# Attention and two dense stages on one core: the outset and the periods of the attention in another order, six PSUM banks for scores, one for values, one for sums

## The chip, the cores and the metric

The kernel runs on one core of a Trainium2 chip. The metric is device time in microseconds (us), the median of the runs; all times below are in us. The engines are TensorE (PE; its weight loads are PEld), VectorE (DVE), ScalarE (ACT), GpSimd (POOL) and SyncE (SP, which here only issues DMAs).

## The reference

Softmax attention with a soft cap, then two dense stages. `B, H, S, D` = 2, 12, 448, 64; 896 tokens of width 768.

```python
scores = cap * np.tanh(scale * (q @ k.T) / cap)
attn = exp(scores - max); attn = attn / (sum(attn) + 1e-09)
x = (attn @ v) as (896, 768)
h = np.maximum(np.maximum(x @ w1, x @ w2), x @ w3)
x = h @ w_out
xn = x / rms(x) * rms_g
out = (silu(xn @ w_gate) * (xn @ w_val)) @ w_out2
```

## The kernel before

The attention is worked in 12 **pairs** of heads, one pair in a **period** of the software pipeline (`period(i)`, i = 0 to 12). Keys are cut into four blocks c = 0 to 3, of 128, 128, 128 and 64 keys; the two heads of a pair lie side by side in the PE array. In period i:

- PE computes the scores of pair i (`scores`, blocks 0 to 2 at L210, each into two PSUM banks, one for each head; block 3 at L217, both heads in one bank), seven banks in all, out of the pool `bank` of five. It then computes the values of pair i-1 (`values`, L247, into one bank of the pool `banko` of two) and the sums of its exponentials over the keys (`sum_all`, L253, two matmuls with a matrix of ones into the one bank `banks`).
- ACT takes the tanh of each score bank (L212, L218), which frees that bank, and then the exponentials of the pair in two instructions (`expo`, L222: e01 of blocks 0 and 1, e23 of blocks 2 and 3).
- POOL adds the exponentials of blocks 0, 1 and 3 (`sum_01` L226, `sum_3` L231), DVE those of block 2 (`sum_2` L235); `sum_all` waits for that.
- DVE divides: `norm(i-2)` takes the reciprocal of the bank of sums (L257) and multiplies the bank of values with it (L259), which frees both; `split_x` (L267, L268) cuts the result into two parts for the dense stage.

Tiles of the PE array have three shapes here, which the rows name: 64\*128 (scores of blocks 0 to 2: 64 rows, 128 columns), 64\*64 (scores of block 3, values of block 3) and 128\*64 (values of blocks 0 to 2, sums).

The dense stages (L277, L531) run as **groups** of 18 matmuls in a fixed list. They need the weights in **units** that are split into a high and a low part (`split_unit`, eight instructions, for units 0 and 1 all on DVE; L109 to L117). Unit 0 is split in period 0, unit 1 in period 1 ahead of the norms, unit 2 in `tail`. `tail` (period 12, the last pair's values) is issued after the 18 matmuls of group 0, so that groups 0, 1 and 2 surround the last values; they use units 0, 1 and 2. Each engine works its instructions in the order in which the program is written (`manual_schedule`); a wait for another engine holds all that stands behind it on its own engine. Banks of the dense stages come from the same three pools in turns of eight (`any_bank`).

Ahead of period 0 stand two **warm** matmuls on zeros (L316) that wait for no data.

Of the kernel before, what the change touches and what calls it, by code (L numbers as in the profile page):

```python
# [8 lines left out]
F32 = mybir.dt.float32  # L9
# [9 lines left out]
B, H, S, D = 2, 12, 448, 64  # L19
NP = H // 2  # L20
P = 128
CP = 112
NC = S // CP
# [17 lines left out]
def attn_moe_kernel(ctx, tc, bounded, qT, kT, v, cap, w123, wo, wgv, wo2, rms_g, out):  # L41
# [17 lines left out]
    def small(name, dt=F32):  # L59
        return tp.tile([P, 512], dt, tag="t", name=name, bufs=NT)  # L60
# [12 lines left out]
        return tp.tile([P, S], F32, tag="xs", name="xs", bufs=NX)  # L73

    def bank():
        return pp.tile([P, 512], F32, tag="b", name="bank", bufs=5)

    def bank_o():
        return pp.tile([P, 512], F32, tag="o", name="banko", bufs=2)

    def bank_s():
        return pp.tile([P, 512], F32, tag="s", name="banks", bufs=1)
# [3 lines left out]
    def any_bank():  # L86

        turn[0] = (turn[0] + 1) % 8
        return (bank_s if turn[0] == 0 else bank_o if turn[0] in (3, 6) else bank)()

# [8 lines left out]
        sp.dma_start(out=mid.rearrange("p a b -> p (a b)").bitcast(U16)[:, :4 * U - 2], in_=src.bitcast(U16)[:, 1:4 * U - 1])  # L99
        return raw[:, :, 1], mid[:, :, 0]  # L100

    def split_unit(words, on_dve):
        hi, lo = (gp.tile([P, U], F32R, tag="g", name=name, bufs=NG) for name in ("whi", "wlo"))
        f = wp.tile([P, U], U32, tag="f", name="f", bufs=2)
        d = wp.tile([P, U], U32, tag="d", name="d", bufs=1)
        high, mid = words
        ff = f.bitcast(F32)
        steps = [
            (lambda: dve.tensor_scalar(f, high, 0x7FFFFFFF, None, op0=ALU.bitwise_and)) if on_dve else  # L109
            (lambda: act.activation(ff, high.bitcast(F32), AF.Abs)),  # L110
            lambda: dve.tensor_scalar(ff, ff, W_MIN, W_MAX, op0=ALU.max, op1=ALU.min),  # L111
            lambda: dve.tensor_scalar(f, f, 3, 0x3FFFF000, op0=ALU.logical_shift_left, op1=ALU.bitwise_and),
            lambda: dve.scalar_tensor_tensor(f, high, 0xC0000000, f, op0=ALU.bitwise_and, op1=ALU.bitwise_or),  # L113
            lambda: (dve.tensor_copy if on_dve else act.copy)(hi, ff),  # L114
            lambda: dve.tensor_scalar(d, f, 0xFF800000, None, op0=ALU.bitwise_and),  # L115
            lambda: dve.tensor_scalar(mid, mid, 0x01FFFFFF, None, op0=ALU.bitwise_and),
            lambda: dve.scalar_tensor_tensor(lo, mid, 2.0 ** -36, d.bitcast(F32), op0=ALU.mult, op1=ALU.mult),  # L117
            load_next,
        ]
        for step in steps:  # L120
            step()
        return hi, lo

    unit_src = [w123[j, n] for j in range(KC) for n in range(3)]
# [7 lines left out]
        if len(loaded) < len(unit_src):  # L132
            loaded.append(load_unit(unit_src[len(loaded)]))

    def split_next():
        i = len(units)
        units.append(split_unit(loaded[i], i < 2))
        loaded[i] = None

    with tc.manual_schedule():  # L140

        pairs = [(b, hp) for b in range(B) for hp in range(NP)]
        n = len(pairs)
        kq, vt, E, EX, Ssum, SB, PO, XS = {}, {}, {}, {}, {}, {}, {}, {}
        X = [None] * KC

        def load_pair(i):
# [88 lines left out]

        def values(i, *blocks):
            for c in blocks:
                if c == 0:
                    PO[i] = bank_o()  # L240
                for j in range(2):
                    if c < KB:
                        w, e = vt[i][:, c * P + j * D:c * P + (j + 1) * D], E[i][c][:, j, :]
                    else:
                        rows = slice(j * KL, (j + 1) * KL)
                        w, e = vt[i][rows, KB * P:], E[i][c][rows]
                    pe.matmul(PO[i][64 * j:64 * j + 64, :S], w, e, start=(c == 0), stop=(c == KB))  # L247

        def sum_all(i):

            ps = SB[i] = bank_s()
            for j in range(2):
                pe.matmul(ps[64 * j:64 * j + 64, :S], ones, Ssum[i][:, j, :], start=True, stop=True)  # L253

        def norm(i):
            r = small("r")[:, :S]
            dve.reciprocal(r, SB.pop(i)[:, :S])  # L257
            xs = XS[i] = spare()
            dve.tensor_mul(xs, PO.pop(i)[:, :S], r)  # L259

        def split_x(i):
            b, hp = pairs[i]
# [49 lines left out]
        dve.memset(warm, 0.0)  # L312
        act.activation(tsc, warm[:, :1], AF.Exp)
        ps = bank()
        for _ in range(2):
            pe.matmul(ps[:, :S], warm[:, :P], warm, start=True, stop=True)  # L316
        load_next()
        load_pair(1)
# [12 lines left out]
        if bounded:  # L331

            guard = const.tile([P, 1], F32, name="guard")
            dve.tensor_scalar_mul(guard, cap_sb, -1.0)
            dve.tensor_tensor(guard, guard, cap_sb, op=ALU.min)
            act.activation(guard, guard, AF.Exp)
            dve.tensor_scalar_mul(guard, guard, 1e-9 / P)
            def period(i):

                if i + 2 < n:
                    load_pair(i + 2)
                    load_v(i + 2)
                if i >= 2:
                    norm(i - 2)
                if i == n:
                    sum_3(i - 1, dve)
                if i >= 1:
                    sum_2(i - 1)  # L350
                if i == 1:
                    split_next()
                if i >= 2:
                    split_x(i - 2)
                if i < n:
                    for c in range(NC):
                        scores(i, c)
                if i >= 1:
                    values(i - 1, 0, 1, 2)
                    sum_all(i - 1)  # L360
                    values(i - 1, 3)
                if i < n:
                    expo(i)
                    if i == 0:

                        split_next()
                        sum_01(i, dve)
                        sum_3(i, dve)
                    else:
                        sum_01(i, dve if i == n - 1 else pool)  # L370
                        if i < n - 1:
                            sum_3(i, pool)

            def tail():
                period(n)
                split_next()
                norm(n - 1)
                split_x(n - 1)

            for i in range(n):  # L380
                period(i)
        else:
            for i in range(n):
                if i + 2 < n:
                    load_pair(i + 2)
                    load_v(i + 2)
                attend(i)
            for _ in range(3):
                split_next()
# [217 lines left out]
```

## Time and profile before

| | us |
|---|---|
| median of 3 runs (lowest, highest) | 554.96 (554.73, 556.86) |
| profiled execution, its own time | 556.08 |
| its span, first to last instruction | 554.3 |
| PE busy | 539.7 (97%) |
| DVE busy | 415.0 (75%) |
| ACT busy | 240.6 (43%) |
| POOL busy | 59.2 (11%) |

The attention takes the first 107 us of the span, up to group 0; the dense stages take the rest. "Granted clock" is the share of TensorE's full clock of 2.4 GHz that it was given: 1.00, or 0.50 for 1.2 GHz. Its record begins at 11.4 us; ahead of that the durations of matmuls tell the level. A matmul of float32 shows as two records (two passes). A busy PE is one with a matmul under way, and not one at its best pace.

### The profile page before, as it was taken

To read this page: it belongs to the slowest core of one execution; us is meant where nothing else is said; L and a number is where in the kernel's file an instruction comes from. 1 tells how busy PE (TensorE), PEld (TensorE's weight loads), DVE (VectorE), ACT (ScalarE), POOL (GpSimd) and SP (SyncE) were. 2 spreads that over 40 slices of the span, in tenths; PEclk is the share of its full clock that TensorE was granted. 3 is DMA by queue.
4 is the path that set the end of the run, shared out by engine and by line. 5 is a ranking of instruction groups with operands and counts; after the bars stand their busy time and mean duration, and the time that the engine had idled before them with its cause. 6 is when DMAs were issued, how large, how long until landed. Compare 5 with 4: busy or idle time off the path is not lost.

```text
span 554.3 us, 7037 instructions
## 1 busy us (share of the span) xinstructions
PE 539.7 (97%) x2682; PEld 438.3 (79%) x2682; DVE 415.0 (75%) x592; ACT 240.6 (43%) x347; POOL 59.2 (11%) x48
## 2 busy tenths in 40 slices
PE   7879999999999999999999999999999999999996
PEld 3223333479889999988998999988888999999996
DVE  4996777799998898686586888878777778836701
ACT  4858898714434333335454333333333333312201
POOL 0335556300000000002122000000000000000000
PEclk9889999999999999999999999999999999999999
DMA  7843320037897878566500476666666666874402
GB/s 256 340 157 100 101 94 6 1 115 246 319 316 287 294 246 278 197 247 229 187 0 1 139 264 245 217 215 207 210 218 223 223 219 217 318 275 173 156 1 105
DMA packets 24810, 105.90 MB, mean 191 GB/s; under 512 B 3008, under 2 KB 9408, under 8 KB 24768
## 3 DMA queue, kind: packets, MB, share of 16 engines
q1 hardware_dynamic: 23760, 104.19, 54.0%
q10 hardware_dynamic: 1008, 1.18, 0.6%
q8 instruction: 23, 0.38, 0.3%
q14 instruction: 19, 0.16, 0.1%
HBM read 102.60 MB, written 2.75 MB: 190 GB/s over the span
## 4 chain that ended last, share of the span: by engine, by line
PE 96%; ACT 1%; DMA 1%; DVE 1%; SPq 0%; issue 0%
PE bank L277 40%; PE banko L277 16%; PE bank L531 10%; PE banko L247 8%; PE banks L277 7%; PE bank L210 6%; PE banko L531 3%; PE banks L531 2%; PE bank L217 2%; PE banks L253 2%; DMA qv<-in_qT 1%; DVE sum L235 1%; ACT e L222 1%; ACT e L212 0%; SPq L600 0%
## 5 line engine op out<-in xcount | busy, mean ns | idle before, releaser
L114 ACT CAST whi<-f 128x768 fp32r<-128x768 f32 x58 | 48.8, 841 | 150.7 <-DVE f L113 127.9
L277 PE MATMUL bank<-xn,whi 128*128 128x512 f32 (+1 forms) x360 | 102.9, 367 | 0.0
L277 PE MATMUL bank<-x,whi 128*128 128x512 f32 (+2 forms) x276 | 79.2, 368 | 0.0
L277 PEld LDWEIGHTS bank<-xn,whi 128*128 128x128 f32 x360 | 66.5, 188 | 8.2
L277 PE MATMUL bank<-xn,wlo 128*128 128x512 f32 (+1 forms) x180 | 66.2, 368 | 0.0
L117 DVE SCALAR_TENSOR_TENSOR wlo<-mid,d 128x768 fp32r<-128x768 uint32 x60 | 58.3, 972 | 5.1 <-PE banks L277 1.6
L113 DVE SCALAR_TENSOR_TENSOR f<-raw,f 128x768 uint32<-128x768 uint32 x60 | 57.5, 959 | 2.1
L277 PEld LDWEIGHTS bank<-x,whi 128*128 128x128 f32 x276 | 51.0, 188 | 7.4 <-issue 1.4
L531 PE MATMUL bank<-whi,a 128*128 128x384 f32 x216 | 54.8, 334 | 0.0
L110 ACT ACTIVATE f<-raw 128x768 f32<-128x768 f32 x58 | 52.6, 907 | 3.5 <-DMA raw<-in_wo 2.5
L277 PE MATMUL bank<-x,wlo 128*128 128x512 f32 (+2 forms) x138 | 50.8, 368 | 0.0
L111 DVE TENSOR_SCALAR f<-f 128x768 f32<-128x768 f32 x60 | 34.8, 581 | 17.4 <-ACT f L110 16.3
L212 ACT ACTIVATE e<-bank,tsc 128x448 f32<-128x448 f32 x72 | 39.3, 642 | 18.8 <-PE bank L210 12.0
L257 DVE RECIPROCAL r<-banks 128x448 f32<-128x448 f32 x12 | 35.5, 2955 | 11.3 <-PE banks L253 11.3
L247 PE MATMUL banko<-e,qv 128*64 128x448 f32 (+1 forms) x192 | 43.2, 572 | 0.0
L277 PE MATMUL banko<-xn,whi 128*128 128x512 f32 (+1 forms) x144 | 40.7, 364 | 0.0
L210 PE MATMUL bank<-qv,k 64*128 64x448 f32 x144 | 37.1, 607 | 2.5 <-ACT e L212 1.9
L531 PEld LDWEIGHTS bank<-whi,a 128*128 128x128 f32 x216 | 39.0, 188 | 0.0
L222 ACT ACTIVATE e<-e,cap_sb 128x1792 f32<-128x1792 f32 (+1 forms) x24 | 37.5, 1633 | 0.0
L115 DVE TENSOR_SCALAR d<-f 128x768 uint32<-128x768 uint32 x60 | 35.5, 592 | 2.0
L277 PEld LDWEIGHTS bank<-xn,wlo 128*128 128x128 f32 x180 | 33.8, 188 | 4.0
L531 PE MATMUL bank<-wlo,a 128*128 128x384 f32 x108 | 36.1, 334 | 0.0
(130 smaller groups left out, 877.7 us busy)
## 6 DMA issues: line engine op xcount, KB each, us to landing
raw<-in_wgv SPq DMA_DIRECT2D x24, 768.0 KB, 4.2
mid<-in_wgv SPq DMA_DIRECT2D x24, 767.5 KB, 5.3
raw<-in_w SPq DMA_DIRECT2D x18, 768.0 KB, 5.2
raw<-in_wo SPq DMA_DIRECT2D x18, 768.0 KB, 4.2
mid<-in_w SPq DMA_DIRECT2D x18, 767.5 KB, 5.6
mid<-in_wo SPq DMA_DIRECT2D x18, 767.5 KB, 5.4
k<-in_kT SPq DMA_DIRECT2D x12, 224.0 KB, 3.1
qv<-in_qT SPq DMA_DIRECT2D x12, 224.0 KB, 3.5
```

Source lines behind the costliest of these rows:

```text
L110: (lambda: act.activation(ff, high.bitcast(F32), AF.Abs)),
L113: lambda: dve.scalar_tensor_tensor(f, high, 0xC0000000, f, op0=ALU.bitwise_and, op1=ALU.bitwise_or),
L114: lambda: (dve.tensor_copy if on_dve else act.copy)(hi, ff),
L115: lambda: dve.tensor_scalar(d, f, 0xFF800000, None, op0=ALU.bitwise_and),
L117: lambda: dve.scalar_tensor_tensor(lo, mid, 2.0 ** -36, d.bitcast(F32), op0=ALU.mult, op1=ALU.mult),
L210: pe.matmul(ps[j][:, :S], k_[rows, c * P:(c + 1) * P], q_[rows], start=True, stop=True)
L212: act.activation(t[:, j, :], ps[j][:, :S], AF.Tanh, scale=tsc)
L222: act.activation(e, e, AF.Exp, scale=cap_sb)
L247: pe.matmul(PO[i][64 * j:64 * j + 64, :S], w, e, start=(c == 0), stop=(c == KB))
L257: dve.reciprocal(r, SB.pop(i)[:, :S])
L277: pe.matmul(ps, a[:, k, :], x[k][h][:, cols], start=(k == 0 and n_ == 0), stop=(k == KC - 1 and n_ == 2))
L531: pe.matmul(acc_o[s][:, :HN], a[:, ts], w[:, sl], start=(k == 0 and n_ == 0), stop=(k == FC - 1 and n_ == 2))
```

## The change

- **Banks**: `bank` six, `banko` one, `banks` one. In the dense stages a bank still comes back after eight groups.
- **Outset**: three warm matmuls. In period 1 the scores of pair 1 and the values of pair 0 are interleaved. The split of unit 1 leaves period 1; its eight instructions and the DMA issue behind them (`load_next`, unit 3) are dealt out, one at the end of `split_x` in each of periods 2 to 8, the last with the issue in period 9.
- **Period**: values in the order 3, 0, 1, then the sums, then block 2.
- **Reciprocals**: the reciprocal of pair i-1 is written at the end of period i, not at the start of period i+1.

```diff
-        return pp.tile([P, 512], F32, tag="b", name="bank", bufs=5)
+        return pp.tile([P, 512], F32, tag="b", name="bank", bufs=6)
-        return pp.tile([P, 512], F32, tag="o", name="banko", bufs=2)
+        return pp.tile([P, 512], F32, tag="o", name="banko", bufs=1)
...
-        return (bank_s if turn[0] == 0 else bank_o if turn[0] in (3, 6) else bank)()
+        return (bank_s if turn[0] == 0 else bank_o if turn[0] == 7 else bank)()
...
+        def recip(i):
+            r = R[i] = small("r")[:, :S]
+            dve.reciprocal(r, SB.pop(i)[:, :S])
+
         def norm(i):
-            r = small("r")[:, :S]
-            dve.reciprocal(r, SB.pop(i)[:, :S])
             xs = XS[i] = spare()
-            dve.tensor_mul(xs, PO.pop(i)[:, :S], r)
+            dve.tensor_mul(xs, PO.pop(i)[:, :S], R.pop(i))
...
-        for _ in range(2):
+        for _ in range(3):
             pe.matmul(ps[:, :S], warm[:, :P], warm, start=True, stop=True)
...
-                if i == 1:
-                    split_next()
                 if i >= 2:
                     split_x(i - 2)
-                if i < n:
-                    for c in range(NC):
-                        scores(i, c)
+
+                    if i == 2:
+                        split_next(steps)
+                    for step in steps[:1 if i < 9 else None]:
+                        step()
+                    del steps[:1 if i < 9 else None]
+                if i == 1:
+                    scores(1, 0)
+                    scores(1, 1)
+                    values(0, 0, 1)
+                    scores(1, 2)
+                    scores(1, 3)
+                    values(0, 3)
+                    sum_all(0)
+                    values(0, 2)
+                else:
+                    if i < n:
+                        for c in range(NC):
+                            scores(i, c)
+                    if i >= 1:
+                        values(i - 1, 3, 0, 1)
+                        sum_all(i - 1)
+                        values(i - 1, 2)
                 if i >= 1:
-                    values(i - 1, 0, 1, 2)
-                    sum_all(i - 1)
-                    values(i - 1, 3)
+                    recip(i - 1)
```

On PE, periods 1 and 2 before (`bank` rows are scores, `banko` rows values, `banks` rows sums; 64x448 in a `bank` row is block 3):

```order
8 L210 MATMUL bank<-qv,k 128x448 x6
9 L217 MATMUL bank<-qv,k 64x448 x2
10 L247 MATMUL banko<-e_139,qv 64x448 x4
11 L247 MATMUL banko<-e_140,qv 64x448 x2
12 L253 MATMUL banks<-sum,ones 64x448 x2
13 L247 MATMUL banko<-e_140,qv 64x448 x2
14 L210 MATMUL bank<-qv,k 128x448 x6
15 L217 MATMUL bank<-qv,k 64x448 x2
16 L247 MATMUL banko<-e_207,qv 64x448 x4
17 L247 MATMUL banko<-e_208,qv 64x448 x2
18 L253 MATMUL banks<-sum,ones 64x448 x2
19 L247 MATMUL banko<-e_208,qv 64x448 x2
```

and now:

```order
8 L213 MATMUL bank<-qv,k 128x448 x4
9 L252 MATMUL banko<-e_140,qv 64x448 x4
10 L213 MATMUL bank<-qv,k 128x448 x2
11 L220 MATMUL bank<-qv,k 64x448 x2
12 L252 MATMUL banko<-e_141,qv 64x448 x2
13 L258 MATMUL banks<-sum,ones 64x448 x2
14 L252 MATMUL banko<-e_141,qv 64x448 x2
15 L213 MATMUL bank<-qv,k 128x448 x6
16 L220 MATMUL bank<-qv,k 64x448 x2
17 L252 MATMUL banko<-e_193,qv 64x448 x2
18 L252 MATMUL banko<-e_192,qv 64x448 x4
19 L258 MATMUL banks<-sum,ones 64x448 x2
```

Values of blocks 0 and 1 moved between the scores of period 1; in period 2 and all later ones block 3 of the values came first and block 2 last, behind the sums.

On DVE, from the last sum of pair 0 into period 2, before:

```order
22 L235 SCALAR_TENSOR_TENSOR sum<-e_140,guard,sum 128x896
23 L109 TENSOR_SCALAR f<-raw 128x768
24 L111 TENSOR_SCALAR f<-f 128x768
25 L112 TENSOR_SCALAR f<-f 128x768
26 L113 SCALAR_TENSOR_TENSOR f<-raw,f 128x768
27 L114 CAST whi<-f 128x768
28 L115 TENSOR_SCALAR d<-f 128x768
29 L116 TENSOR_SCALAR mid<-mid 128x768
30 L117 SCALAR_TENSOR_TENSOR wlo<-mid,d 128x768
31 L257 RECIPROCAL r<-banks 128x448
32 L259 TENSOR_TENSOR xs<-banko,r 128x448
33 L235 SCALAR_TENSOR_TENSOR sum<-e_208,guard,sum 128x896
```

and now:

```order
22 L238 SCALAR_TENSOR_TENSOR sum<-e_141,guard,sum 128x896
23 L262 RECIPROCAL r<-banks 128x448
24 L266 TENSOR_TENSOR xs<-banko,r 128x448
25 L238 SCALAR_TENSOR_TENSOR sum<-e_193,guard,sum 128x896
26 L274 CAST x<-xs 128x448
27 L275 TENSOR_TENSOR x<-xs,x 128x448
28 L109 TENSOR_SCALAR f<-raw 128x768
29 L262 RECIPROCAL r<-banks 128x448
```

The eight instructions of unit 1's split left the place ahead of pair 0's reciprocal, and one stands ahead of each later reciprocal.

On DVE, in `tail` (last pair; L111 to L117 are the split of unit 2), before:

```order
85 L235 SCALAR_TENSOR_TENSOR sum<-e_750,guard,sum 128x896
86 L267 CAST x<-xs 128x448
87 L268 TENSOR_TENSOR x<-xs,x 128x448
88 L111 TENSOR_SCALAR f<-f 128x768
89 L112 TENSOR_SCALAR f<-f 128x768
90 L113 SCALAR_TENSOR_TENSOR f<-raw,f 128x768
91 L115 TENSOR_SCALAR d<-f 128x768
92 L116 TENSOR_SCALAR mid<-mid 128x768
93 L117 SCALAR_TENSOR_TENSOR wlo<-mid,d 128x768
94 L257 RECIPROCAL r<-banks 128x448
95 L259 TENSOR_TENSOR xs<-banko,r 128x448
```

and now:

```order
85 L238 SCALAR_TENSOR_TENSOR sum<-e_751,guard,sum 128x896
86 L274 CAST x<-xs 128x448
87 L275 TENSOR_TENSOR x<-xs,x 128x448
88 L262 RECIPROCAL r<-banks 128x448
89 L111 TENSOR_SCALAR f<-f 128x768
90 L112 TENSOR_SCALAR f<-f 128x768
91 L113 SCALAR_TENSOR_TENSOR f<-raw,f 128x768
92 L115 TENSOR_SCALAR d<-f 128x768
93 L116 TENSOR_SCALAR mid<-mid 128x768
94 L117 SCALAR_TENSOR_TENSOR wlo<-mid,d 128x768
95 L266 TENSOR_TENSOR xs<-banko,r 128x448
```

The last pair's reciprocal moved from behind the split of unit 2 to ahead of it.

## Rows read from the trace of the kernel before

**Rows 1.** Windows: stretch, length, busy PE, PEld, DVE, ACT, POOL, clock, DMA, GB/s.

```profile
15.00:18.24 3.24, 1.33 (x5) 0.49 (x6) 2.81 (x4) 3.24 (x6) 0.00 (x0) 1.00 1.05 401
18.24:21.65 3.41, 3.41 (x10) 0.77 (x8) 3.27 (x6) 3.41 (x5) 0.00 (x0) 0.50 1.01 422
...
30.60:35.30 4.70, 0.94 (x8) 0.24 (x6) 4.60 (x4) 1.77 (x2) 3.95 (x3) 1.00 0.92 343
...
45.46:107.08 61.62, 61.62 (x291) 22.45 (x289) 45.66 (x42) 54.07 (x73) 33.74 (x24) 1.00 0.18 57
...
122.38:554.30 431.92, 426.73 (x2193) 392.00 (x2191) 320.74 (x498) 154.73 (x232) 13.73 (x11) 1.00 0.60 208
```

**Rows 2.** Timeline of PE, outset: start, us, line, tiles, shape, records, idle before.

```profile
3.16 3.33 PE L316 MATMUL bank<-warm 128*128 128x448 f32 x4 [3.16 <-DVE warm L312]
7.12 4.64 PE L210 MATMUL bank<-qv,k 64*128 64x448 f32 x12 [0.63 <-DMA qv<-in_qT]
...
34.38 0.97 PE L253 MATMUL banks<-sum,ones 128*64 128x448 f32 x4 [3.76 <-DVE sum L235]
```

**Rows 3.** Timeline of ACT, outset.

```profile
8.98 1.16 ACT L212 ACTIVATE e<-bank,tsc 128x448 f32<-128x448 f32 x2 [1.76 <-PE bank L210]
...
16.32 3.26 ACT L212 ACTIVATE e<-bank,tsc 128x448 f32<-128x448 f32 x6
...
20.06 3.09 ACT L222 ACTIVATE e<-e,cap_sb 128x1792 f32<-128x1792 f32 x2
```

**Rows 4.** Timeline of DVE and of POOL, outset.

```profile
22.07 2.45 DVE L115 TENSOR_SCALAR d<-f 128x768 uint32<-128x768 uint32 x1
...
31.25 2.98 DVE L235 SCALAR_TENSOR_TENSOR sum<-e,guard,sum 128x896 f32<-128x896 f32 x1
...
21.92 2.19 POOL L226 TENSOR_TENSOR sum<-e 128x896 f32<-128x896 f32 x1 [18.90 <-ACT e L222]
```

**Rows 5.** Timeline of PE, one steady period.

```profile
53.16 2.82 PE L210 MATMUL bank<-qv,k 64*128 64x448 f32 x12
55.91 0.97 PE L217 MATMUL bank<-qv,k 64*64 64x448 f32 x4
56.81 2.48 PE L247 MATMUL banko<-e,qv 128*64 128x448 f32 x12
59.11 0.92 PE L253 MATMUL banks<-sum,ones 128*64 128x448 f32 x4
59.96 0.97 PE L247 MATMUL banko<-e,qv 64*64 64x448 f32 x4
```

**Rows 6.** Timeline, narrow windows in that period: PE from 54.96, ACT from 54.27.

```profile
54.96 1.02 PE L210 MATMUL bank<-qv,k 64*128 64x448 f32 x3
...
54.27 1.16 ACT L212 ACTIVATE e<-bank,tsc 128x448 f32<-128x448 f32 x2 [0.94 <-POOL sum L226]
```

**Rows 7.** Timeline of DVE and of POOL, the same period.

```profile
52.41 2.96 DVE L257 RECIPROCAL r<-banks 128x448 f32<-128x448 f32 x1 [1.31 <-PE banks L253]
55.47 0.62 DVE L259 TENSOR_TENSOR xs<-banko,r 128x448 f32<-128x448 f32 x1
56.68 1.15 DVE L235 SCALAR_TENSOR_TENSOR sum<-e,guard,sum 128x896 f32<-128x896 f32 x1 [0.59 <-POOL sum L231]
...
58.17 0.63 DVE L268 TENSOR_TENSOR x<-xs,x 128x448 fp32r<-128x448 f32 x1
...
52.17 2.08 POOL L226 TENSOR_TENSOR sum<-e 128x896 f32<-128x896 f32 x1 [3.22 <-ACT e L222]
```

**Rows 8.** Timeline of DVE, ACT, PE around `tail`: split of unit 2, group 2.

```profile
116.08 0.56 DVE L115 TENSOR_SCALAR d<-f 128x768 uint32<-128x768 uint32 x1
...
117.15 0.96 DVE L117 SCALAR_TENSOR_TENSOR wlo<-mid,d 128x768 fp32r<-128x768 uint32 x1
...
116.08 0.84 ACT L114 CAST whi<-f 128x768 fp32r<-128x768 f32 x1 [8.06 <-DVE f L113]
...
118.73 0.57 PE L277 MATMUL banko<-x,whi 128*128 128x448 f32 x2
```

More of the change, by code (lines that the diff above doesn't have):

```diff
@@ L100, in load_unit, with split_unit @@
         return raw[:, :, 1], mid[:, :, 0]
-    def split_unit(words, on_dve):
+    def split_unit(words, on_dve, defer=None):
         hi, lo = (gp.tile([P, U], F32R, tag="g", name=name, bufs=NG) for name in ("whi", "wlo"))
@@ L119, in split_unit @@
         ]
-        for step in steps:
-            step()
+        if defer is None:
+            for step in steps:
+                step()
+        else:
+            defer.extend(steps)
         return hi, lo
@@ L133, in load_next, with split_next @@
             loaded.append(load_unit(unit_src[len(loaded)]))
-    def split_next():
+    def split_next(defer=None):
         i = len(units)
-        units.append(split_unit(loaded[i], i < 2))
+        units.append(split_unit(loaded[i], i < 2, defer))
         loaded[i] = None
@@ L143, in attn_moe_kernel @@
         n = len(pairs)
-        kq, vt, E, EX, Ssum, SB, PO, XS = {}, {}, {}, {}, {}, {}, {}, {}
+        kq, vt, E, EX, Ssum, SB, PO, R, XS, done = {}, {}, {}, {}, {}, {}, {}, {}, {}, {}
         X = [None] * KC
@@ L238, in values @@
             for c in blocks:
-                if c == 0:
+                first = i not in PO
+                if first:
                     PO[i] = bank_o()
+                done[i] = done.get(i, 0) + 1
                 for j in range(2):
@@ L246, in values @@
                         w, e = vt[i][rows, KB * P:], E[i][c][rows]
-                    pe.matmul(PO[i][64 * j:64 * j + 64, :S], w, e, start=(c == 0), stop=(c == KB))
+                    pe.matmul(PO[i][64 * j:64 * j + 64, :S], w, e, start=first, stop=(done[i] == NC))
         def sum_all(i):
@@ L337, in attn_moe_kernel @@
             dve.tensor_scalar_mul(guard, guard, 1e-9 / P)
+            steps = []
             def period(i):
@@ L350, in period @@
                     sum_2(i - 1)
-                if i == 1:
-                    split_next()
                 if i >= 2:
                     split_x(i - 2)
-                if i < n:
-                    for c in range(NC):
-                        scores(i, c)
+                    if i == 2:
+                        split_next(steps)
+                    for step in steps[:1 if i < 9 else None]:
+                        step()
+                    del steps[:1 if i < 9 else None]
[8 more added lines that the diff above has]
+                    values(0, 2)
+                else:
+                    if i < n:
[5 more added lines that the diff above has]
+                        values(i - 1, 2)
                 if i >= 1:
-                    values(i - 1, 0, 1, 2)
-                    sum_all(i - 1)
-                    values(i - 1, 3)
+                    recip(i - 1)
                 if i < n:
```

## The prediction

> **What bounds the kernel now.** I read the windows first. From 122.38 to the end PE is busy 426.73 of 431.92 us [rows 1]; the change leaves that part as it is, since a bank there comes back after eight groups before and now. So the change is worth what it moves the start of group 3, at 122.38. Ahead of it are three stages, each with its own limit.
>
> The outset, up to 45.46: the timeline of PE shows what ends each wait. From 15.00 to 18.24 PE is busy 1.33 us [rows 1], because the scores of pair 1 wait for banks that ACT frees; from 30.60 to 35.30 it is busy 0.94 us, and the wait before 34.38 ends on DVE's sum [rows 1, 2]. After each of the two comes a stretch at granted clock 0.50 (18.24 to 21.65 stands for both) [rows 1].
>
> Eight steady periods, 45.46 to 107.08: PE is busy all 61.62 us [rows 1], 7.70 each. A busy PE can still hold waits; the starts in one period show them. And the tail, 107.08 to 122.38, where groups 0 to 2 and the last values share PE.
>
> **The outset.** The third warm matmul holds PE some 1.5 longer than 6.49 (two took 3.33 [rows 2]; a pass lasts 0.75 at the low clock), so pair 0's scores start near 7.75, not at 7.12. But the 0.63 gap is gone, and PE then works without a break from 3.16. Before, these scores took 4.64 for 12 records, against 2.82 in a steady period [rows 2, 5]: low clock nearly to the end. I take the rise at about 8, so that the first tanh stays near 8.98 [rows 3] and pair 0's further scores no longer hold up ACT. Bounds: 0.5 earlier, or no earlier rise at all, then 1.2 later.
>
> From there ACT sets the pace. One pair's tanh and exponentials, fed without waits, last 6.83 (16.32 to 20.06 + 3.09 [rows 3]). So pair 1's tanh starts at 8.98 + 6.83 = 15.8 (before 16.32), pair 2's at 22.6, if PE is there. It is: e01 of pair 0 ends near 14.4, and then come values 0 and 1, the rest of pair 1's scores, value 3, the sums and value 2, seven blocks of 0.75 to 0.95 [rows 5], some 5.9. Pair 2's scores start at 20.3, the first is ready 1.1 later, ahead of 22.6.
>
> The removed stall: DVE no longer has the split of unit 1 ahead of pair 0's reciprocal; beside POOL's add its instructions ran up to 2.45 and the sum at 31.25 ran 2.98, against 1.15 in a steady period [rows 4, 7]. Next late for pair 1's sums is POOL: e01 of pair 1 ends at 21.3, and from POOL's first add to DVE's last sum it is 56.68 - 52.17 = 4.51 [rows 7]. The sum ends at 27.1, the ones-matmuls start at 27.25, pair 3's scores at 28.9, and after one period with a short wait on the value bank period 4 starts at 36.3. **Gain 45.46 - 36.3 = 9.2.** Bounds: 7.4 (clock not early, or a low-clock stretch in period 1, where PE still idles over 1 us) and 10.2 (ACT sets the pace through period 3).
>
> Unit 3's load goes behind the loads of all pairs on SP. Unit 3 is split after group 1, some 20 us later, so this costs nothing; pair 4's loads, which stood behind unit 3's, come earlier.
>
> **The period.** Starts 53.16, 55.91, 56.81, 59.11, 59.96 and 60.86 (53.16 + 7.70) [rows 5]: score blocks 2.75, score block 3 0.90, values 2.30 for three blocks (0.77 each, no change of tile shape), sums 0.85, value 3 0.90.
> - Sixth bank: the sixth score matmul starts at 54.96, right after the first tanh, 54.27 + about 0.63 [rows 6]: there PE waits for a bank. With six banks it follows its neighbour, and I count 2.75 - 2.30 - 0.15 = 0.30 gained; the seventh tile then needs the bank of the first tanh, free long before.
> - Order: the shape changes four times in a period, now three times. Into and out of value 3 it cost 0.08 + 0.13 in the sums and the value, and about 0.15 in the next scores, together 0.36. The new change, 128\*64 to 64\*128, is not in the trace: between 0 and 0.36; half of it, 0.18, by the nearest row, the mean of the four. Gain 0.18.
>
> PE would need 7.70 - 0.30 - 0.18 = 7.22. The Trainium skill, TensorEngine Tiling (Array Packing), Key Properties, says that a change of tiling mode drains the engine; the rows agree as far as each change shows 0.1 to 0.2. It prices no change; by it the new one costs one drain like the others, 7.22 again.
>
> A new loop: with one value bank, value 3 waits for the multiply, which waits for the reciprocal, for the sums, for value 3. Value 3 0.90, two blocks 1.54, sums to reciprocal 1.00 (59.11 to 60.11), reciprocal to multiply 3.06, multiply 0.62, to PE 0.14 (sum's end 34.23 to 34.38) [rows 2, 4, 5, 7]: 7.26. So 7.27 is the period, PE and the loop level. Queued behind a waiting value 3 on PE are the sums and the next scores, and ACT behind these; ACT's 6.83 leaves 0.4.
>
> The dealt-out steps (0.56 each, two of 0.96 [rows 8]) stand between `split_x`, which ends at 58.80, and the reciprocal at 60.11 [rows 7]: 1.31 of idle, 0.88 at the shorter period. Six are hidden; I charge 0.35 for each of the two long ones. **Gain 8 x 0.43 - 0.7 = 2.7**; bounds 1.2 (7.45, with the loop late) and 4.4 (7.05, the new change free and the loop faster).
>
> **The tail.** Group 0 takes 3.84; value 3 now waits for the multiply of pair 10, behind pair 11's add: 0.3 late. Worse, DVE meets the last reciprocal before the split of unit 2. It must wait for the last sums, which now end 7.6 after group 0's start (4.2, then value 3, two blocks, the sums), and lasts 2.96 [rows 7], so the split starts at 10.65. Its six instructions take some 4.2: four of 0.56 and two of 0.96 [rows 8]. Before, it had ended at 118.11, or 11.04 after the start of group 0 at 107.07, just ahead of group 2 at 118.73, 11.66 [rows 8]. Now the third of the six ends at 12.8, ACT's cast of the high part (0.84 [rows 8]) at 13.7 and the low part at 14.85. Group 2, due at 12.0, waits 1.7 for the high part and, two matmuls on, 0.8 for the low. **Loss 0.3 + 2.5 = 2.8**; bounds 1.5 and 3.5. All dense groups stand behind it, with nothing to hide it. 2.5 us of idle in 3.2 is like the idle at 15.00 to 18.24, after which 3.41 us ran at 0.50 [rows 1]: at half pace that is **1.7** more. It may fail to come: 0 to 1.7.
>
> **Sum.** 9.2 + 2.7 - 2.8 - 1.7 = 7.4 off. The profiled execution took 556.08, 1.78 over its span of 554.3, and lies 1.1 above the median; a like execution afterwards would show a span near 546.9. Off the median, 554.96 - 7.4 = **547.5**.
>
> **The rivals.**
> - *No low clock in the tail*: 545.8. For it: the idle is in two pieces. Against it: the stretch after 15.00.
> - *The period hardly shortens*: the loop or the new shape change keeps it at 7.55, and the gain is 8 x 0.15 - 0.7: 2.2 less, 549.7. This is also the case that the sixth bank's wait was another's. For it: the loop stands level with PE. Against it: the start at 54.96 follows the tanh so closely. An outset without the early clock gives much the same time, 548.7.
> - *Slower: the dealt-out steps meet POOL's add.* The row of 2.45 against 0.56 began 0.15 after POOL's add [rows 4, 8]. A step that starts behind POOL's add would take 1.9 more, and reciprocal, multiply, value 3 and PE with it, less 0.2 of slack: 8 x 1.7 = 13.6, and 547.5 + 13.6 = 561. It decides at POOL's start: 52.17 + 7.27 = 59.44 against a step at 58.80 [rows 7], 0.64 to spare. A long step under way is not touched (the row at 21.92 began inside a DVE instruction). The Trainium skill, GPSIMD Engine Reference, Specifications, says that POOL shares its SBUF interfaces with DVE, with contention for two-port modes and for two SBUF inputs, which the steps are; the rows agree by the 2.45, and the reciprocal from PSUM shows none (2.96).
>
> **How the numbers follow.** Forecast 0.45; no low clock 0.25; period or outset short of it 0.20; steps meet POOL 0.04; other 0.06. The first three span 545.8 to 549.7; with the bounds of the outset, 545.0 to 550.0 for 8 in 10. About 0.5% (2.8 us) is what a measurement here can tell from no change: faster below 552.2. All of the first three lie there: faster 0.93, same 0.04, slower 0.03.
>
> **What would show it.** Period 4's scores (the fifth block of scores) at 36 to 37; periods of 7.2 to 7.4 with no matmul waiting for the first tanh; no DVE instruction over 1.5 in the outset apart from reciprocals; group 2 waiting 1.5 to 2 for the high part of unit 2, a second wait behind it, and a granted clock of 0.50 soon after; group 3's start at 115 (113.3 without the low clock). Wrong would be a step beside POOL of over 2 us, periods over 7.5, or a split of unit 2 that does not hold PE.

## The result, and the profile after

The median is 545.71 us (545.37 to 546.91, six runs) against 554.85 for the kernel before, timed beside it: a ratio of 0.985 (95% interval 0.982 to 0.988). The forecast was 547.5 (545.0 to 550.0). The profiled execution took 545.37, with a span of 543.6, 1.77 less than its time (1.78 in the kernel before).

Stage by stage, as starts on PE in the two profiled executions:

| stage | before, us | after, us | forecast gain | measured gain |
|---|---|---|---|---|
| outset, to the scores of period 4 | 45.46 | 35.77 | 9.2 | 9.69 |
| eight periods, to group 0 | 61.62 | 58.38 | 2.7 | 3.24 |
| tail, group 0 to group 3 | 15.30 | 17.77 | -2.8 | -2.47 |
| low clock behind the tail | | none | -1.7 | 0 |
| group 3 to the end | 431.92 | 431.68 | 0 | 0.24 |

The sum is 10.7 of span. Of that 9.1 is left between the medians, because the profiled execution of before lay 1.2 above the median of its kernel and that of after 0.3 below.

The windows of after (columns as in [rows 1]) show the second and the last stage; PE is busy without a break in the periods again, and the dense part is what it was:

```profile
35.77:94.15 58.38, 58.38 (x290) 20.62 (x289) 48.75 (x47) 53.85 (x73) 34.19 (x24) 1.00 0.28 87
...
111.92:543.60 431.68, 426.70 (x2193) 391.98 (x2191) 318.48 (x494) 154.68 (x232) 13.74 (x11) 1.00 0.60 208
```

**Outset.** Timeline of PE in after, for [rows 2]:

```profile
3.15 4.62 PE L323 MATMUL bank<-warm 128*128 128x448 f32 x6 [3.15 <-DVE warm L319]
7.70 2.53 PE L213 MATMUL bank<-qv,k 64*128 64x448 f32 x12
...
26.68 0.97 PE L258 MATMUL banks<-sum,ones 128*64 128x448 f32 x4 [0.56 <-DVE sum L238]
```

Pair 0's scores start at 7.70 without a gap and take 2.53 where they took 4.64: the granted clock rose at 7.45 (before at 11.41). The wait ahead of pair 1's sums fell from 3.76 to 0.56. ACT, for [rows 3], goes in steps of 6.6:

```profile
8.76 3.25 ACT L215 ACTIVATE e<-bank,tsc 128x448 f32<-128x448 f32 x6 [1.60 <-PE bank L213]
...
15.37 3.29 ACT L215 ACTIVATE e<-bank,tsc 128x448 f32<-128x448 f32 x6
...
21.97 3.34 ACT L215 ACTIVATE e<-bank,tsc 128x448 f32<-128x448 f32 x6
...
29.39 3.26 ACT L215 ACTIVATE e<-bank,tsc 128x448 f32<-128x448 f32 x6 [0.57 <-PE bank L213]
```

The tanh of pairs 1 and 2 start behind ACT's own work; that of pair 3 waits for PE again, and from there PE sets the pace.

**One steady period.** PE, for [rows 5]:

```profile
35.77 2.53 PE L213 MATMUL bank<-qv,k 64*128 64x448 f32 x12
38.22 0.97 PE L220 MATMUL bank<-qv,k 64*64 64x448 f32 x4
39.03 2.57 PE L252 MATMUL banko<-e,qv 64*64 64x448 f32 x12
41.43 0.92 PE L258 MATMUL banks<-sum,ones 128*64 128x448 f32 x4
42.18 0.92 PE L252 MATMUL banko<-e,qv 128*64 128x448 f32 x4
43.03 2.53 PE L213 MATMUL bank<-qv,k 64*128 64x448 f32 x12
...
46.29 2.57 PE L252 MATMUL banko<-e,qv 64*64 64x448 f32 x12
```

From start to start the scores take 2.45 (before 2.75), block 3 0.81 (0.90), the values 3, 0, 1 2.40, the sums 0.75, value 2 0.85: 7.26 (before 7.70). DVE, for [rows 7]:

```profile
41.55 0.56 DVE L112 TENSOR_SCALAR f<-f 128x768 uint32<-128x768 uint32 x1
42.42 2.96 DVE L262 RECIPROCAL r<-banks 128x448 f32<-128x448 f32 x1 [0.32 <-PE banks L258]
45.49 0.62 DVE L266 TENSOR_TENSOR xs<-banko,r 128x448 f32<-128x448 f32 x1
...
49.04 0.95 DVE L113 SCALAR_TENSOR_TENSOR f<-raw,f 128x768 uint32<-128x768 uint32 x1
```

A short step of the split (41.55) ends 0.3 us before the reciprocal can start. A long one (49.04) takes up that gap. The multiply ends at 46.11, value 3 starts at 46.29.

**Tail.** DVE, ACT and PE around group 2, for [rows 8]:

```profile
101.50 2.96 DVE L262 RECIPROCAL r<-banks 128x448 f32<-128x448 f32 x1 [0.20 <-PE banks L258]
...
107.56 0.96 DVE L117 SCALAR_TENSOR_TENSOR wlo<-mid,d 128x768 fp32r<-128x768 uint32 x1
...
106.49 0.83 ACT L114 CAST whi<-f 128x768 fp32r<-128x768 f32 x1 [10.95 <-DVE f L113]
...
107.38 0.68 PE L284 MATMUL bank<-x,whi 128*128 128x448 f32 x2 [1.33 <-ACT whi L114]
108.57 0.47 PE L284 MATMUL bank<-x,wlo 128*128 128x448 f32 x1 [0.52 <-DVE wlo L117]
...
111.92 0.57 PE L284 MATMUL bank<-x,whi 128*128 128x448 f32 x2
```

Group 2 waits twice, for the high part and then for the low part of unit 2, each behind the last reciprocal.

### The profile page after: what moved, and what is told of

Read it like the earlier page. It is cut to its first block, busy times and chain, and to the rows that moved or that the text cites. A ratio compares the mean times of both kernels' runs of the same rounds, so it can differ in the third digit from the quotient of the medians.

```text
span 543.6 us, 7034 instructions
## 1 busy us (share of the span) xinstructions
PE 531.6 (98%) x2684; PEld 434.6 (80%) x2684; DVE 407.0 (75%) x592; ACT 240.1 (44%) x347; POOL 58.5 (11%) x48
## 3 DMA queue, kind: packets, MB, share of 16 engines
q10 hardware_dynamic: 1008, 1.18, 0.6%
HBM read 102.60 MB, written 2.75 MB: 194 GB/s over the span
## 4 chain that ended last, share of the span: by engine, by line
PE 94%; ACT 2%; DVE 2%; POOL 1%; DVEq 0%; issue 0%
PE bank L284 48%; PE bank L556 11%; PE banko L284 8%; PE banks L284 7%; PE banko L252 6%; PE bank L213 4%; PE banks L556 2%; PE banko L556 2%; PE banks L258 2%; PE bank L220 1%; ACT e L215 1%; ACT e L225 1%; PE bank L323 1%; DVE r L262 1%; POOL sum L234 0%; POOL sum L229 0%
## 5 line engine op out<-in xcount | busy, mean ns | idle before, releaser
L284 PE MATMUL bank<-xn,whi 128*128 128x384 f32 (+1 forms) x432 | 121.4, 362 | 0.0
L284 PE MATMUL bank<-x,whi 128*128 128x512 f32 (+2 forms) x336 | 95.3, 364 | 1.3 <-ACT whi L114 1.3
L284 PEld LDWEIGHTS bank<-xn,whi 128*128 128x128 f32 x432 | 79.5, 188 | 8.4
L284 PE MATMUL bank<-xn,wlo 128*128 128x512 f32 (+1 forms) x216 | 78.3, 363 | 0.0
L284 PEld LDWEIGHTS bank<-x,whi 128*128 128x128 f32 x336 | 62.0, 188 | 9.6 <-ACT whi L114 1.7
L117 DVE SCALAR_TENSOR_TENSOR wlo<-mid,d 128x768 fp32r<-128x768 uint32 x60 | 57.5, 959 | 5.9 <-PE banks L284 2.8
L284 PE MATMUL bank<-x,wlo 128*128 128x512 f32 (+2 forms) x168 | 61.3, 365 | 0.5 <-DVE wlo L117 0.5
L556 PE MATMUL bank<-whi,a 128*128 128x384 f32 x240 | 60.8, 334 | 0.0
L111 DVE TENSOR_SCALAR f<-f 128x768 f32<-128x768 f32 x60 | 34.8, 580 | 17.9 <-ACT f L110 16.8
L284 PEld LDWEIGHTS bank<-xn,wlo 128*128 128x128 f32 x216 | 40.5, 188 | 4.0
L112 DVE TENSOR_SCALAR f<-f 128x768 uint32<-128x768 uint32 x60 | 33.6, 560 | 2.0
L284 PEld LDWEIGHTS bank<-x,wlo 128*128 128x128 f32 x168 | 31.5, 188 | 4.0 <-DVE wlo L117 0.9
```

The costliest lines, as they stand in the source:

```text
L284: pe.matmul(ps, a[:, k, :], x[k][h][:, cols], start=(k == 0 and n_ == 0), stop=(k == KC - 1 and n_ == 2))
L556: pe.matmul(acc_o[s][:, :HN], a[:, ts], w[:, sl], start=(k == 0 and n_ == 0), stop=(k == FC - 1 and n_ == 2))
```

## The experiments

Each edit is against the kernel after. Times are medians, to be set against 545.71. The kernel before was timed again beside each of three sets of runs, with medians of 554.76, 555.02 and 556.36; the kernel after was not. So differences of 1 us or less are read from the stages of the profiles, not from the medians.

**The tail's order.** Does the last reciprocal ahead of the split of unit 2 cost what it seems to? In this run it alone goes back behind the split.

```diff
-                if i >= 1:
+                if 1 <= i < n:
                     recip(i - 1)
...
                 split_next()
+                recip(n - 1)
                 norm(n - 1)
```

> The changed kernel with one thing undone: in the tail the last pair's reciprocal stands behind the split of unit 2 again. Theory: the reciprocal ahead of the split is what makes group 2 wait; it held the split back until the last sums and for 2.96 us more. Then group 2 follows group 1 without a wait for the high part (1.3 us in the changed kernel) or the low part (0.5), group 3 starts at 109.5 instead of 111.9, and the time is 543.3. Rival: group 2 is late because the last values wait for the single value bank; then the reciprocal's place does nothing, group 3 stays at 111.9 and the time at 545.7.

Measured: 543.4 (543.35 to 543.97, six runs; ratio to before 0.981, 0.978 to 0.984), span 541.7. DVE and PE of this kernel:

```profile
104.68 0.96 DVE L117 SCALAR_TENSOR_TENSOR wlo<-mid,d 128x768 fp32r<-128x768 uint32 x1
105.56 2.95 DVE L262 RECIPROCAL r<-banks 128x448 f32<-128x448 f32 x1
...
106.10 0.57 PE L284 MATMUL bank<-x,whi 128*128 128x448 f32 x2
```

The split ends before group 2 is due, and nothing waits: from group 0 (94.37) to group 3 (109.75) 15.38, as before the change. The tail's loss is this one move, 2.4 us in the profiles and 2.3 in the medians.

**The split of unit 1 back in one piece**, in period 1, ahead of pair 0's reciprocal, and with it the DMA issue of unit 3; all else stays.

```diff
+                if i == 1:
+                    split_next()
                 if i >= 2:
                     split_x(i - 2)
...
-                    if i == 2:
-                        split_next(steps)
-                    for step in steps[:1 if i < 9 else None]:
-                        step()
-                    del steps[:1 if i < 9 else None]
```

> The changed kernel with the split of unit 1 whole in period 1 again, ahead of pair 0's reciprocal, all else as changed. Theory: the dealt-out split is what took the stall out of the outset. The last three instructions of the split fall beside POOL's add and run 1.5 to 2.5 us each, pair 0's reciprocal starts near 27 instead of 19.5, and value 3 of pair 1 waits for its bank until about 31; period 4 starts at 42 to 44 instead of 35.8 and the time is 552 to 555. Rival: the outset gained by the early clock and the interleaved period 1; then period 4 starts within 1 us of 35.8 and the time stays within 545 to 547.

Measured: 555.18 (553.54 to 556.04, eight runs; ratio 1.001, 0.999 to 1.004). DVE, PE and POOL in period 2 of this kernel, and two windows:

```profile
23.37 2.72 DVE L117 SCALAR_TENSOR_TENSOR wlo<-mid,d 128x768 fp32r<-128x768 uint32 x1
26.01 2.94 DVE L262 RECIPROCAL r<-banks 128x448 f32<-128x448 f32 x1
...
29.74 4.16 PE L252 MATMUL banko<-e,qv 64*64 64x448 f32 x12 [3.63 <-DVE xs L266]
...
22.93 2.35 POOL L229 TENSOR_TENSOR sum<-e 128x896 f32<-128x896 f32 x1 [19.94 <-ACT e L225]
...
13.54:16.95 3.41, 3.41 (x10) 1.43 (x12) 3.27 (x6) 3.08 (x5) 0.00 (x0) 0.50 1.02 407
115.94:119.35 3.41, 3.41 (x11) 3.03 (x10) 3.27 (x7) 0.00 (x0) 0.00 (x0) 0.50 0.83 315
```

Pair 0's reciprocal starts at 26.01 (after: 19.54), its multiply frees the one value bank only at 29.68, and PE idles 3.63 there. Period 4 starts at 43.09, 7.32 later. A stretch at granted clock 0.50 follows the idle one (30.60 to 34.02).

Not all of the loss is the split's. The stretch at 13.54 stands ahead of the split, which starts at 19.07; it follows a wait of 2.58 for pair 1's load (1.19 in after). Unit 0's load came 1.06 later than in after, too, and so the split itself started some 1.0 late. Of the 7.32, then, 6.3 to 7.3 is the split's, by my estimate from these rows. The other 1.6 of the 9.0 in the spans is the low clock at 115.94, behind the stall of the tail, which the split does not touch (group 0 to group 3 took 19.33). With this edit undone the change shows no gain over the kernel before, by the split and the low clock together. The way of the loss differs, too: with the one value bank pair 1's values waited, while in the kernel before its sums did (3.76, [rows 2]).

**Five banks for scores, two for values**, as before, in the new order.

```diff
-name="bank", bufs=6)
+name="bank", bufs=5)
-name="banko", bufs=1)
+name="banko", bufs=2)
...
-bank_o if turn[0] == 7 else bank
+bank_o if turn[0] in (3, 6) else bank
```

> The changed kernel with the banks of before: five for scores, two for values, one for sums. Theory: the sixth score matmul waits again for the first tanh in each period; 0.25 more a period, 7.50 to 7.52 instead of 7.27, and 1.5 to 2 us in all, 547.3 to 547.7. The second value bank gives back less than 0.4, since value 3 waits for its bank only where a long step stands ahead (0.1 in two periods). Rival 1: the period gained by the order alone; it stays at 7.27 and the time at 545.7. Rival 2: the loop over the one value bank sets the period; with two it falls below 7.2.

Measured: 548.13 (547.83 to 550.65, five runs). PE:

```profile
43.93 2.82 PE L213 MATMUL bank<-qv,k 64*128 64x448 f32 x12
46.67 0.97 PE L220 MATMUL bank<-qv,k 64*64 64x448 f32 x4
...
51.48 0.65 PE L213 MATMUL bank<-qv,k 64*128 64x448 f32 x2
```

The scores take 2.74 again and the period 7.55: the sixth bank, less what the second value bank gives back, is worth 0.29 a period. Over the eight periods it is 2.06 (60.44 against 58.38), since the two of 7.40 in after (see below) take 7.55 as well. The other 0.6 of the 2.7 in the spans lies ahead of period 4 (36.37), 0.4 of it in the first tanh (9.14 against 8.76, the clock rose at 8.33).

**The values in the old order**, 0, 1, 2, sums, 3, with the new banks.

```diff
-                        values(i - 1, 3, 0, 1)
+                        values(i - 1, 0, 1, 2)
                         sum_all(i - 1)
-                        values(i - 1, 2)
+                        values(i - 1, 3)
```

> The changed kernel with the values of periods 2 and on in the order of before: 0, 1, 2, the sums, then 3; banks six and one as changed. Theory: four changes of tile shape in a period instead of three. With five and two banks the period was 7.55 against 7.27, so the sixth bank is worth 0.29 and the order what is left of 7.70 - 7.27, that is 0.14: the period is 7.41, group 0 starts 1.1 later than 94.15, and the time is 546.8. Rival: the order is worth nothing by its shapes but makes the sums early for the reciprocal; with the single value bank the loop then sets the period, and it is 7.6 or more, 548.5 or later.

Measured: 548.1 (547.69 to 548.7, four runs). PE, one period, and a window of the tail:

```profile
50.75 2.53 PE L213 MATMUL bank<-qv,k 64*128 64x448 f32 x12
...
58.16 2.53 PE L213 MATMUL bank<-qv,k 64*128 64x448 f32 x12
...
109.90:113.31 3.41, 3.41 (x11) 3.01 (x10) 3.27 (x7) 0.00 (x0) 0.00 (x0) 0.50 0.84 299
```

7.41: the order is worth 0.15 a period, 0.91 over the eight (59.29 against 58.38); group 0 starts 1.07 later (95.22 against 94.15). In the profiled execution (547.69) the rest is not the order's: behind the stall of the tail, which this kernel has too, a stretch at 0.50 came here (109.90 to 113.31), and from the start of group 2 to that of group 3 it took 6.10, not 4.54. For the median that is not shown: another of the four runs took 547.88 at a mean granted clock of 0.999, and one such stretch alone would bring the mean to 0.997. That run was not profiled; what held it stays open.

**Two warm matmuls**, as before.

```diff
-        for _ in range(3):
+        for _ in range(2):
```

> The changed kernel with two warm matmuls as before. Theory: with the pause of 0.6 us ahead of the first scores back, the granted clock rises only near 10 to 11.5 instead of 7.4, pair 0's later scores hold up ACT, and pair 1's tanh starts 0.6 to 1.2 us later; period 4 starts at 36.4 to 37 and the time is 546.2 to 547. Rival: ACT and the DMAs of pair 1 set the pace in any case; pair 1's tanh starts within 0.2 of 15.4, and the time stays at 545.7 or falls by the 0.6 us that the third matmul took.

Measured: 547.71 (546.74 to 548.98, six runs). PE and ACT, and two windows of the tail:

```profile
7.49 4.17 PE L213 MATMUL bank<-qv,k 64*128 64x448 f32 x12 [1.03 <-DMA qv<-in_qT]
...
9.36 1.16 ACT L215 ACTIVATE e<-bank,tsc 128x448 f32<-128x448 f32 x2 [1.50 <-PE bank L213]
...
106.40:109.80 3.40, 1.62 (x7) 0.84 (x6) 3.30 (x6) 2.07 (x3) 0.00 (x0) 1.00 0.33 69
109.82:113.23 3.41, 3.41 (x10) 3.02 (x11) 3.27 (x7) 0.00 (x0) 0.00 (x0) 0.50 0.96 344
```

The clock rises at 10.83, the first tanh starts 0.6 later, and period 4 starts at 36.84, 1.07 later. The rest of the 2.5 in the spans is the low clock behind the tail's stall once more (group 2 to group 3 took 6.10). In after the stall itself was no shorter:

```profile
105.90:108.60 2.70, 0.85 (x4) 0.33 (x3) 2.63 (x5) 2.08 (x3) 0.00 (x0) 1.00 0.34 68
```

but the clock stayed at 1.00 behind it. Over all twelve profiles the rise came at 6.71 to 9.21 with three warm matmuls (ten kernels) and at 10.83 and 11.41 with two.

**Scores and values of period 1 not interleaved.**

```diff
-                    scores(1, 0)
-                    scores(1, 1)
-                    values(0, 0, 1)
-                    scores(1, 2)
-                    scores(1, 3)
-                    values(0, 3)
+                    for c in range(NC):
+                        scores(1, c)
+                    values(0, 3, 0, 1)
```

> The changed kernel with period 1 like the later ones: all scores of pair 1, then values 3, 0, 1, the sums, value 2. Theory: ACT sets the pace of the outset (tanh and exponentials of pairs 0 to 2 without a gap from 8.8 to 28.7) and POOL's adds of pair 1 the start of period 3, so the interleaving is worth little: block 3 of the scores waits for the first tanh of pair 1, period 2 starts 0.5 to 1 later than 20.18, but pair 2's tanh within 0.3 of 21.97, period 4 within 0.4 of 35.8, 545.7 to 546.2; more only where PE's idle time there is followed by a low clock. Rival: the interleaving keeps ACT fed; without it pair 2's tanh and period 4 are 1 to 2 us later, 547 to 548.

Measured: two runs, 546.4 and 548.21, which settle nothing. The profile says more. ACT and PE:

```profile
9.47 3.26 ACT L215 ACTIVATE e<-bank,tsc 128x448 f32<-128x448 f32 x6 [2.28 <-PE bank L213]
...
22.69 3.35 ACT L215 ACTIVATE e<-bank,tsc 128x448 f32<-128x448 f32 x6
...
16.81 0.97 PE L220 MATMUL bank<-qv,k 64*64 64x448 f32 x4 [1.98 <-ACT e L215]
```

PE does wait 1.98 for a bank, but ACT takes 13.22 from the first to the third tanh, as in after (13.21). All of the 0.7 by which period 4 is later (36.48) is there in the first tanh already (9.47 against 8.76, the clock rose at 8.99). So the interleaving hid idle time of PE that cost nothing in this profile.

**The steps of the split later**, behind the reciprocal, so that they should meet POOL's add: the rival that ended slower.

```diff
                 if i >= 2:
                     split_x(i - 2)
-                    if i == 2:
-                        split_next(steps)
-                    for step in steps[:1 if i < 9 else None]:
-                        step()
-                    del steps[:1 if i < 9 else None]
...
                     recip(i - 1)
+                if i >= 2:
+                    if i == 2:
+                        split_next(steps)
+                    for step in steps[:1 if i < 9 else None]:
+                        step()
+                    del steps[:1 if i < 9 else None]
```

> The changed kernel with each dealt-out step behind the period's reciprocal instead of ahead of it, so that it meets POOL's adds. Theory (the slower rival of the prediction): a step beside POOL's add lasts until that add ends, 1.2 to 2.4 us instead of 0.56 or 0.96, and the multiply, value 3 and PE are late by that less some 0.2; periods of 8.3 to 9.4 while there are steps, and 8 to 14 us in all, 554 to 560. Rival: no contention; a step costs its own 0.56 less the slack, periods of 7.6 to 7.8, and 3 to 4 us in all, 549 to 550.

Measured: 548.8 (two runs, 548.69 and 548.91). DVE and POOL:

```profile
53.55 0.90 DVE L113 SCALAR_TENSOR_TENSOR f<-raw,f 128x768 uint32<-128x768 uint32 x1
...
61.34 0.50 DVE L114 CAST whi<-f 128x768 fp32r<-128x768 f32 x1
...
52.48 2.95 POOL L234 TENSOR_TENSOR sum<-sum,e 64x448 f32<-64x448 f32 x2
...
60.15 2.67 POOL L234 TENSOR_TENSOR sum<-sum,e 64x448 f32<-64x448 f32 x2
```

The theory failed here: the eight steps took 0.50 to 1.14, not 1.2 to 2.4. The step came around the gap between POOL's two adds, and it was the second add that was held off (behind the step at 53.55 it took 1.77 and not 1.13; the two take 2.53 to 2.95, in after 2.31). Periods were 7.40 to 7.80 and once 8.06, with the long step at 83.81, since the step also delays the multiply.

**The steps inside POOL's add**: between the multiply of `norm` and `sum_2`.

```diff
-                if i >= 1:
-                    sum_2(i - 1)
                 if i >= 2:
-                    split_x(i - 2)
-
                     if i == 2:
                         split_next(steps)
...
                     del steps[:1 if i < 9 else None]
+                if i >= 1:
+                    sum_2(i - 1)
+                if i >= 2:
+                    split_x(i - 2)
```

> The changed kernel with each dealt-out step between the multiply and DVE's last sum, some 0.1 to 0.2 us after the start of one of POOL's adds of block 3 (1.15 each), and not just ahead of one or between two. Theory 1: whichever of the two engines starts first holds the other off until its own instruction ends. Then a step that starts inside an add lasts until the add is over, 1.2 to 1.7 us instead of 0.56 or 0.96, and DVE's last sum, which waits for that add anyway, is late by 0.6 to 1.0; this delay is within the slack ahead of the ones-matmuls, so the time stays within 0.7 of 545.7. Theory 2: DVE is not held off by an add of 64 partitions, only by the wide one of 128 partitions; steps last 0.56 to 0.8 and nothing moves.

Measured: 546.22 (two runs, 545.97 and 546.48). DVE and POOL:

```profile
46.30 1.74 DVE L113 SCALAR_TENSOR_TENSOR f<-raw,f 128x768 uint32<-128x768 uint32 x1
...
53.80 1.12 DVE L114 CAST whi<-f 128x768 fp32r<-128x768 f32 x1
...
44.91 2.31 POOL L234 TENSOR_TENSOR sum<-sum,e 64x448 f32<-64x448 f32 x2
...
52.19 2.32 POOL L234 TENSOR_TENSOR sum<-sum,e 64x448 f32<-64x448 f32 x2
```

Now the steps that start inside an add are slow (0.55 in after becomes 1.12, 0.95 becomes 1.74) and the add is not. The slow steps end 0.82 (46.30) and 0.41 (53.80) after the add's end at 47.22 and 54.51; that is most of their length, so most of their work is done when it is over. Group 0 starts only 0.48 later than in after (94.63), because `sum_2` has to wait for POOL at this place anyway.

**The outset alone**: the tail, the banks and the order of the values as before; the warm matmul, the order of period 1, the dealt-out split and the early reciprocals stay. The edit is those of the three runs above (tail, banks, values) together.

> The changed outset alone: three warm matmuls, period 1 interleaved, the split of unit 1 dealt out; five, two and one banks, the values in the order 0, 1, 2, sums, 3, and the last reciprocal behind the split of unit 2, all as before. Theory: the parts add up. The outset gives 9.0 to 9.7: period 4 starts at 36.0 to 36.5; the periods are 7.70 again, group 0 starts 61.6 later, near 97.9, group 3 near 113.2, and the time is 546.4 to 547.2. Rival: the parts don't add, since the steps or the banks of before spoil the outset too; period 4 later than 37.5 or periods over 7.8, 548 or more.

Measured: 547.49 (546.83 to 547.69, four runs). Period 4 starts at 37.15, a period is 7.70 as before, the tail 15.39. The clock rose late (9.21): of the 1.4 by which period 4 is later than in after, 0.9 is there in the first tanh (9.62 against 8.76). From period 4 to group 0 it is 61.62, 3.24 more than in after; the banks (2.06) and the order (0.91), each undone alone, make 2.97 of that. So the parts add up. Against the kernel before, timed beside it (556.36), this run is 8.9 faster: nearly the whole gain is the outset's, since what the periods win (3.24) the tail all but loses (2.47).

**A version that is better**: the tail's order put right, and pair 1's add of block 3 on DVE instead of POOL, whose chain the sums of pair 1 still waited for (0.56 in after).

```diff
-                if i == n:
+                if i in (2, n):
                     sum_3(i - 1, dve)
...
-                if i >= 1:
+                if 1 <= i < n:
                     recip(i - 1)
...
-                        if i < n - 1:
+                        if 1 < i < n - 1:
                             sum_3(i, pool)
...
                 split_next()
+                recip(n - 1)
```

> The changed kernel with the last reciprocal behind the split of unit 2 (543.4 alone) and, beside that, block 3 of pair 1's sum added on DVE in period 2, behind the multiply, where DVE waited 2.1 us for POOL. Theory: the sums of pair 1 wait 0.6 us for POOL and DVE, and period 3 starts that much late; DVE has block 3 added about 1 us ahead of POOL, the wait goes, period 3 starts at 27.8 to 28.0 instead of 28.3 to 28.5, and the time is 542.9. Rival: something else holds period 3 (ACT's tanh, value 3 of pair 2 waiting for its bank); the time stays at 543.4.

Measured: 543.17 (542.69 to 544.98, six runs; ratio to before 0.980, 0.977 to 0.983), span 540.9. PE and DVE:

```profile
27.90 2.53 PE L213 MATMUL bank<-qv,k 64*128 64x448 f32 x12
...
52.80 0.62 DVE L266 TENSOR_TENSOR xs<-banko,r 128x448 f32<-128x448 f32 x1 [0.53 <-PE bank L213]
```

Pair 3's scores start 0.44 sooner than in after, without a wait. At group 0 the lead is 0.16, since one multiply then waited 0.53 for PE, which I could not explain. One of the six runs (544.98, mean clock 0.997) is longer by 1.4 than the next. The version beats both kernels, but not measurably the run with the tail alone (543.4).

## Why the prediction was right, and by how much it missed

**The outset: right, 9.69 for 9.2.** The mechanism was the forecast one: no split ahead of pair 0's reciprocal, so no low clock after the idle stretches, and the early clock. The run with the whole split prices the first at 6.3 to 7.3 at period 4 and the run with two warm matmuls the second at 1.1. The terms were off by the clock, which rose at 7.45 and not at 8, and by ACT, which takes 6.6 from tanh to tanh and not 6.83: that sum ran to the end of the last exponential, and the next tanh starts before it (in after at 21.97, with the end at 22.17). POOL's chain was next late, as said: pair 1's sums waited for it, but only 0.56. The interleaving, which the prediction used to show that PE is in time, turned out to be worth nothing at period 4. A low clock in period 1, the lower bound of this stage, did not come; of the ten profiles with three warm matmuls one, that of the whole split, has it there, ahead of anything that its edit touches.

**The periods: right, 3.24 for 2.7.** 0.30 for the sixth bank measured 0.29, 0.18 for the order measured 0.15, and 7.27 for the period 7.26 to 7.27. PE and the loop over the one value bank are level to 0.04, as said: between the multiply's end at 46.11 and value 3 at 46.29 lies 0.18, of which 0.14 is the way to PE. So the long steps were seen: the periods from 50.30 and from 79.49 took 7.40. But that is 0.14 each, not 0.35: this was the mis-sized term, 0.4 of the 0.5 missed. The bounds of this gain, 1.2 and 4.4, come to 1.3 and 4.5 by their own periods of 7.45 and 7.05. The Trainium skill, TensorEngine Tiling (Array Packing), Key Properties, has each change of mode drain the engine; the order with one change fewer gained 0.15 in the trace, which agrees.

**The tail: right, 2.47 for 2.8.** The two waits of group 2 were 1.33 and 0.52 where 1.7 and 0.8 were forecast. The last sums ended 7.30 after group 0's start (101.45), not 7.6, because value 3 hardly waited (under 0.1, not 0.3). Putting the one reciprocal back gave it all back.

**The low clock behind it: the step that failed.** I took 1.7 as the likeliest, for the stall is like the one at 15.00 in [rows 1]. In the profiled execution it did not come, and the median is near the first rival, 545.8. Yet it exists. The profiles of three kernels with the same stall (split whole, two warm, old order of values) show it; those of five others, after's among them, do not. The length of the stall does not decide: the two waits of group 2 sum to 1.70 to 1.85 where the low clock came, and to 1.78 to 1.86 where it did not. Two of the six runs of after were 1.3 longer than the rest (546.81 and 546.91), at a mean clock of 0.994 and 0.995 over the run, where the rest had 0.999 to 1.0. They were not profiled, so that their stretch lay in the tail is likely but not shown. In the run with the tail alone, which has no stall there, the six runs lie within 0.6. The size was about right (1.4 to 1.6 in the profiles against 1.7); the chance was too high. What decides between the two I have not found.

**The rivals.** That the period hardly shortens: no, 7.26. That the steps meet POOL: not in this kernel, whose step at 41.55 ends 0.4 before POOL's add at 42.48. The mechanism is real where a step starts inside an add, as the run with the steps inside the add shows, but no run had the case that was priced at 13.6, a step that starts behind POOL's wide add and ahead of the reciprocal. Steps moved to other places cost 0.5 and 3.1. The price of one such step, 1.9, is borne out: in the run with the whole split the step at 23.37, just behind the start of the wide add, took 2.72 and not 0.96.

The span forecast, 546.9, was 3.3 above the 543.6 measured: 0.5 outset, 0.5 periods, 0.3 tail, 1.7 clock, 0.2 dense part. By medians only 1.8 is left, as before's profiled execution was 1.2 above its kernel's median and after's 0.3 below. That this cancels part of the miss is luck. The kernel before is the one that varies: beside the experiments its runs lay between 551.85 and 557.11, at mean clocks of 0.989 to 0.999, so it too has low stretches in some runs and not in others; one profile of it could not show that. A gain worked out from one profile's low-clock stretches is a gain against that run.

## What to carry to other kernels

Look at who stands first in an engine's order, not only at how busy it is: eight instructions of DVE ahead of one reciprocal held 6 to 7 us of this kernel, and one reciprocal ahead of six instructions 2.4. When a step is moved earlier everywhere in a loop, look at the last turn by itself, for there another user may be waiting behind it. And put small steps of one engine into its known gaps, measured from start to start; a gap of 0.9 hid steps of 0.56 and let 0.14 through of those of 0.96.

## What the hardware showed

- DVE and POOL exclude each other, first come, for these instructions, which read and write SBUF alone. A DVE step that starts inside a POOL add waits for its end: 46.30 in the run with the steps inside the add, and in the run with the whole split 23.37, of 2.72, which ends 0.81 after the add of 22.93 to 25.28. A POOL add behind a running step waits for the step: 1.77 and not 1.13 in the run with the steps later. The reciprocal, from PSUM, shows none of it (2.94 to 2.97 in all). The Trainium skill, GPSIMD Engine Reference, Specifications, speaks of contention between the two, with DVE instructions in a 2-port mode or with two SBUF inputs; the trace agrees and gives the amounts. Steps with one input waited as well (the cast at 53.80); whether they ran in such a mode no run shows.
- Much the same stall of PE, two waits of 1.18 to 1.34 and 0.51 to 0.53, was followed by 3.41 us at granted clock 0.50 in the profiles of three kernels and not in those of five.
- Three warm matmuls and no gap ahead of the first scores had the clock rise at 6.71 to 9.21 in ten profiles; two, with a gap of 0.63 and 1.03, at 11.41 and 10.83.
